# Six of nine tap products computed as even and odd halves with pairwise-summed weights

## The chip, the core and the metric

The kernel runs on one core of one Trainium2 chip. A core has a matrix engine (TensorE, PE in the profile, with its weight loads as PEld), two elementwise engines (VectorE, DVE; ScalarE, ACT), GpSimd (POOL), SyncE (SP), which here only issues DMAs, and 16 DMA engines that move data between the main memory and SBUF. PE writes its sums to PSUM, which has 8 banks of 128 x 512 float32; DVE and ACT read them from there. The metric is the device time of one execution in microseconds (us), lower is better.

## The reference

A causal dilated convolution over time with 15 taps and dilation 2, a gate, and a projection:

```python
B, T, D, K = (2, 4000, 512, 15)      # x: (B, T, D), w: (K, D, 2*D), w_o: (D, D), all bf16
pad = (K - 1) * 2
xp = jnp.pad(x, ((0, 0), (pad, 0), (0, 0)))
h = sum(einsum('btc,cd->btd', xp[:, pad - 2*i : pad - 2*i + T, :], w[i]) for i in range(K))
z = tanh(h[..., :D]) * sigmoid(h[..., D:])
out = z @ w_o
```

So each output row is a sum of 15 matrix products of 512 x 1024, then an elementwise gate, then one product of 512 x 512.

## The kernel before

**Streams.** Time is cut by its remainder modulo 8 into rows of 500 (NK): row r holds the times 8k + r. Because the dilation is 2, the even remainders (p = 0) and the odd ones (p = 1) never mix. A *supertile* is one batch entry and one p; there are 4. Inside it lie four streams U0 to U3, and the 15 taps fall into four phases of at most 4 taps (l = 0 to 3; tap 4l + e belongs to phase e, and tap 15 does not exist).

**Nine products.** A 4 x 4 polyphase filter would take 16 sub-filters. The kernel takes nine, by summing streams and weights first: a, b, c work on U0, U2, U02 = U0 + U2; d, e, f on U1, U3, U13; g, hh, ii on U01, U23, U0123. The weights for c, f, g, hh and ii are sums of taps, called slabs. The function `product` forms one of them in one PSUM bank: for each tap l and each 128-channel block cc one weight load and one matmul of 128 x 501 (500 columns and one more on the left), 16 in all; product e has three taps, 12. DVE combines the nine with additions and subtractions (p1, q1, A1, p2, q2, B1, s, s3, C0, qg, C1 and the four sums H0 to H3); ACT copies the products a, d, g from PSUM to SBUF first and later applies tanh (`th`) or sigmoid (`sg`).

**Loops.** The 512 channels of f and of g are done in four passes (dc) of 128 each, since the summed weights of more would not fit. In each pass the four supertiles follow each other, and each is done twice: hf = 0 gives the tanh half, hf = 1 the sigmoid half and z. One such piece is called a *unit* here: 4 passes x 4 supertiles x 2 halves = 32 units of 8 x 16 + 12 = 140 matmuls. In pass 0 the streams are made: by transposes on PE for the first supertile, by DMA transposes for the others, with four-row remainders by PE (`pt`); the five sums are made by DVE (line 219). They are written to main memory (`xsp`) and read back in passes 1 to 3. z is written to `zsp`; in the last pass `make_outproj_steps` reads it back and multiplies by w_o (`po`, line 353, 256 matmuls), ACT casts, SP stores.

**Weights.** `make_weight_steps` loads 15 taps per pass in two halves of 128 columns (128 KB each) and forms 18 summed slabs per half (line 151). For pass 0 POOL issues the loads and DVE adds; for passes 1 to 3 SP issues and POOL adds, all of it during the last unit of the pass before.

**What sets the order.** The code lists work per product and attaches the loads, sums and spills of the next supertile or pass as *hooks* behind a given product. When the program is built, a scheduler with its own costs orders the instructions of each engine; on the chip each engine then runs its own list strictly in that order and waits on semaphores. Tiles come from pools with a fixed number of buffers: a new tile waits until an old one has been read for the last time. What the change touches sits at `product` (line 258), the copies at lines 289, 300 and 321, `act_out` (lines 273 to 282), `produce_sum` (219), `reload` (223), the spill (240) and the hooks at the end.

Of the kernel before, what the change touches and what calls it, by code (L numbers as in the profile page):

```python
# [12 lines left out]
def kernel(  # L13
# [21 lines left out]
    assert K <= 16 and T % 8 == 0  # L35
# [8 lines left out]
    NREM = NK - NT16  # L44

# [34 lines left out]
    XORDER = [XNAME[pn] for pn in PRODS]  # L80

# [5 lines left out]
    wsl_pool = ctx.enter_context(tc.tile_pool(name="wsl", bufs=33 + 3))  # L87
    xin_pool = ctx.enter_context(tc.tile_pool(name="xin", bufs=9 + 2))
    pcopy_pool = ctx.enter_context(tc.tile_pool(name="pcopy", bufs=3))
    ctmp_pool = ctx.enter_context(tc.tile_pool(name="ctmp", bufs=3))  # L90
    keep_pool = ctx.enter_context(tc.tile_pool(name="keep", bufs=7))
    hpre_pool = ctx.enter_context(tc.tile_pool(name="hpre", bufs=3))
    th_pool = ctx.enter_context(tc.tile_pool(name="th", bufs=5))
    sg_pool = ctx.enter_context(tc.tile_pool(name="sg", bufs=2))
    z_pool = ctx.enter_context(tc.tile_pool(name="z", bufs=8))
# [3 lines left out]
    for (b, p) in supertiles:  # L99
        for n in XORDER:  # L100
            xsp[(b, p, n)] = dram.tile([P, CC, XU], bf16, name=f"xsp_{b}_{p}_{n}", tag=f"xsp_{b}_{p}_{n}")
# [23 lines left out]
    def make_weight_steps(dc, sum_eng, dma_eng):  # L125
        wo = {}
        slabs = {pn: [None] * NL for pn in PRODS}
        sums = {}
# [14 lines left out]
        def slab_add(pn, l, A, Bm, h):  # L143
            if A is None or Bm is None:
                slabs[pn][l] = A if Bm is None else Bm
                return
            if h == 0:
                t = wsl_pool.tile([P, CC, 2 * P], bf16, name=f"w{pn}{l}_p{dc}", tag="wsl")
                slabs[pn][l] = t
            t = slabs[pn][l]  # L150
            sum_eng.tensor_tensor(t[:, :, halfs(h)], A[:, :, halfs(h)], Bm[:, :, halfs(h)], ALU.add)  # L151

        def step_orig(pn, e):
            def fn(h):
                for l in range(NL):
                    load_orig(4 * l + e, h)
                    slabs[pn][l] = get_orig(4 * l + e)
            return fn

        def step_sum(pn, e0, e1):  # L160
            def fn(h):
                for l in range(NL):
                    slab_add(pn, l, get_orig(4 * l + e0), get_orig(4 * l + e1), h)
            return fn

        def step_ii(h):
            for l in range(NL):
                slab_add("ii", l, slabs["g"][l], slabs["hh"][l], h)
# [7 lines left out]
        return slabs, steps  # L176

    def make_x_steps(dc, b, p, sum_eng, use_dmat=False):
# [7 lines left out]
        def pe_rows(t, rows, k0, ksz, pt, slot, copy_eng):  # L186
            xn = xnat_pool.tile([P, D], bf16, name="xn", tag="xn")
            nc.sync.dma_start(xn[:ksz, :], rows[k0:k0 + ksz, :])  # L188
            for cc in range(CC):
# [6 lines left out]

        def produce_base(q):
# [279 lines left out]
```

## Time and profile before

| what | value |
|---|---|
| median of 4 runs | 1029.59 us (1028.81 to 1030.4) |
| the profiled execution's own time | 1029.43 us |
| its span (first to last instruction) | 1027.6 us |
| granted TensorE clock, mean | 0.999 |
| PE busy | 1016.1 us (99%), 4848 matmuls |
| DVE busy | 407.5 us (40%) |
| ACT busy | 177.0 us (17%) |
| POOL busy | 161.4 us (16%) |
| moved by DMA | 121.81 MB, 119 GB/s on the mean |

The span is the part that the trace shows; 1.83 us of the execution's time lie around it. In a row of the timeline the first number is the start in us from the span's start, the second how long the merged group lasted, then engine, line, operation, tiles and shape, and at the end the count. In a group's row the numbers behind the bar are the busy time of all in us, the mean of one in ns, and the idle time before them with what ended it. The duration of a matmul in the trace is a modelled one, from its start to when its result stands; matmuls overlap, so the pace of a stream is the difference of starts, not that duration.

### The profile page before, as it was taken

To read this page: it belongs to the slowest core of one execution; us is meant where nothing else is said; L and a number is where in the kernel's file an instruction comes from. 1 tells how busy PE (TensorE), PEld (TensorE's weight loads), DVE (VectorE), ACT (ScalarE), POOL (GpSimd) and SP (SyncE) were. 2 spreads that over 40 slices of the span, in tenths; PEclk is the share of its full clock that TensorE was granted. 3 is DMA by queue.
4 is the path that set the end of the run, shared out by engine and by line. 5 is a ranking of instruction groups with operands and counts; after the bars stand their busy time and mean duration, and the time that the engine had idled before them with its cause. 6 is when DMAs were issued, how large, how long until landed. Compare 5 with 4: busy or idle time off the path is not lost.

```text
span 1027.6 us, 12121 instructions
## 1 busy us (share of the span) xinstructions
PE 1016.1 (99%) x4848; PEld 472.2 (46%) x4848; DVE 407.5 (40%) x620; ACT 177.0 (17%) x298; POOL 161.4 (16%) x160
## 2 busy tenths in 40 slices
PE   6999999999999999999999999999999999999998
PEld 3444444444444444444444444444444544544444
DVE  3854443635533242433434343342544133223132
ACT  2111011111111111111011111111112312312214
POOL 8100000007900000004920000003850000000000
PEclk9999999999999999999999999999999999999999
DMA  9996672917543250608625060425615425323303
GB/s 241 233 227 97 152 134 62 230 26 175 159 123 88 62 144 21 164 22 185 175 81 161 23 182 2 134 73 138 191 42 148 137 62 156 108 84 104 98 1 95
DMA packets 174868, 121.81 MB, mean 119 GB/s; under 512 B 77276, under 2 KB 173852, under 8 KB 174812
## 3 DMA queue, kind: packets, MB, share of 16 engines
q1 hardware_dynamic: 173372, 117.11, 45.6%
q0 software_dynamic: 1440, 3.93, 1.5%
q8 instruction: 38, 0.62, 0.3%
q14 instruction: 18, 0.15, 0.0%
HBM read 81.56 MB, written 33.36 MB: 112 GB/s over the span
## 4 chain that ended last, share of the span: by engine, by line
PE 99%; DMA 1%; SPq 0%; ACT 0%; issue 0%
PE ps_a L258 11%; PE ps_c L258 11%; PE ps_b L258 11%; PE ps_f L258 11%; PE ps_d L258 11%; PE ps_hh L258 11%; PE ps_ii L258 11%; PE ps_g L258 11%; PE ps_e L258 8%; PE po L353 5%; PE pt L190 1%; DMA xn<-in_x_dram 1%; SPq L188 0%; ACT o_sb L360 0%
## 5 line engine op out<-in xcount | busy, mean ns | idle before, releaser
L258 PEld LDWEIGHTS <-wo_p 128*128 128x128 bf16 x2176 | 210.5, 97 | 248.9 <-issue 0.5
L258 PE MATMUL ps_a<-xU,wo_p 128*128 128x501 bf16 x512 | 114.3, 376 | 0.0
L258 PE MATMUL ps_c<-xU,wc_p 128*128 128x501 bf16 x512 | 114.2, 375 | 0.0
L258 PE MATMUL ps_d<-xU,wo_p 128*128 128x501 bf16 x512 | 114.2, 374 | 0.0
L258 PE MATMUL ps_b<-xU,wo_p 128*128 128x501 bf16 x512 | 113.9, 375 | 0.0
L258 PE MATMUL ps_ii<-xU,wii_p 128*128 128x501 bf16 x512 | 113.8, 374 | 0.0
L258 PE MATMUL ps_g<-xU,wg_p 128*128 128x501 bf16 x512 | 113.8, 374 | 0.0
L151 POOL TENSOR_TENSOR wc_p<-wo_p,wo_p 128x512 bf16<-128x512 bf16 x24 | 26.9, 1152 | 427.3 <-PE ps_b L258 426.4
L303 DVE TENSOR_TENSOR p<-d_sb,ps_e 128x500 f32<-128x500 f32 x32 | 21.7, 677 | 177.7 <-PE ps_e L258 177.7
L258 PE MATMUL ps_f<-xU,wf_p 128*128 128x501 bf16 x384 | 86.8, 375 | 0.0
L258 PE MATMUL ps_e<-xU,wo_p 128*128 128x501 bf16 x384 | 86.8, 375 | 0.0
L258 PE MATMUL ps_hh<-xU,whh_p 128*128 128x501 bf16 x384 | 86.8, 375 | 0.0
L292 DVE TENSOR_TENSOR p<-a_sb,ps_b 128x500 f32<-128x500 f32 x32 | 21.7, 677 | 148.9 <-PE ps_b L258 148.9
L273 ACT ACTIVATE th<-H 128x500 f32<-128x500 f32 x64 | 39.3, 620 | 224.9 <-DVE H L312 110.9
L277 ACT ACTIVATE sg<-H 128x500 f32<-128x500 f32 x64 | 39.3, 621 | 224.4 <-DVE H L312 117.4
L258 PEld LDWEIGHTS <-wg_p 128*128 128x128 bf16 x512 | 49.6, 97 | 59.0
L258 PEld LDWEIGHTS <-wii_p 128*128 128x128 bf16 x512 | 49.6, 97 | 59.0
L258 PEld LDWEIGHTS <-wc_p 128*128 128x128 bf16 x512 | 49.3, 97 | 57.8
L300 ACT COPY d_sb<-ps_d 128x501 f32<-128x501 f32 x32 | 18.5, 577 | 280.0 <-PE ps_d L258 280.0
L324 DVE TENSOR_TENSOR C<-g_sb,ps_hh 128x500 f32<-128x500 f32 x32 | 21.7, 677 | 92.2 <-PE ps_hh L258 92.1
L279 DVE TENSOR_TENSOR zt<-th,sg 128x500 bf16<-128x500 f32 x64 | 48.5, 777 | 24.1 <-ACT sg L277 23.4
L258 PEld LDWEIGHTS <-whh_p 128*128 128x128 bf16 x384 | 37.2, 97 | 44.3
(48 smaller groups left out, 763.0 us busy)
## 6 DMA issues: line engine op xcount, KB each, us to landing
xU<-xsp_U SPq DMA_DIRECT2D x108, 516.0 KB
xsp_U<-xU SPq DMA_DIRECT2D x36, 516.0 KB
wo_p<-in_w_dram SPq DMA_DIRECT2D x90, 128.0 KB
zsp<-zt SPq DMA_DIRECT2D x48, 125.0 KB
zl<-zsp SPq DMA_DIRECT2D x48, 125.0 KB
out_dram<-o_sb SPq DMA_DIRECT2D x32, 126.0 KB
wo_p<-in_w_dram POOLq DMA_DIRECT2D x30, 128.0 KB, 7.3
out_dram<-o_sb SPq DMA_DIRECT2D x16, 128.0 KB
```

The source lines that it names most:

```text
L151: sum_eng.tensor_tensor(t[:, :, halfs(h)], A[:, :, halfs(h)], Bm[:, :, halfs(h)], ALU.add)
L190: nc.tensor.transpose(pt[:, slot, cc, 0:ksz], xn[:ksz, cc * P:(cc + 1) * P], ident[:ksz, :ksz])
L258: nc.tensor.matmul(ps[:, :], lhsT=slabs[pn][l][:, cc, hf * P:(hf + 1) * P], rhs=xtile[:, cc, st:st + NP1], start=(idx == 0), stop=(idx == ...
L273: nc.scalar.activation(th[:], H[:, K1], AF.Tanh)
L277: nc.scalar.activation(sg[:], H[:, K1], AF.Sigmoid)
L279: V.tensor_tensor(zt[:], state["th"][q][:], sg[:], ALU.mult)
L292: V.tensor_tensor(r["p1"][:, K1], r["a_sb"][:, K1], ps[:, KSH], ALU.add)
L300: nc.scalar.copy(r["d_sb"][:, ALLC], ps[:, ALLC])
L303: V.tensor_tensor(r["p2"][:, K1], r["d_sb"][:, K1], ps[:, KSH], ALU.add)
L324: V.tensor_tensor(r["C0"][:, K1], r["g_sb"][:, K1], ps[:, KSH], ALU.add)
L353: nc.tensor.matmul(po[:ksz, :], lhsT=zs[dcp][:, k0:k0 + ksz], rhs=wo_sb[:, dcp, :], start=(dcp == 0), stop=(dcp == HC - 1),)
```

## The change

Six of the nine products (a, c, d, f, g, ii) are no longer 16 matmuls of 501 columns. Each stream they use is split again, by the parity of k, into three half-length pieces kept in one tile of the pool `xh`: `o` (the odd-indexed columns), `m` (even minus the odd one after) and `n` (even minus the odd one before). Their taps are grouped in pairs, and the sums of two neighbouring taps are new slabs (`slabs2`, tiles with `_2` in the name). A split product is then three pieces of 2 taps x 4 blocks = 8 matmuls of 251 columns:

1. the pair sums times `o`, into bank ps_o; ACT copies it to SBUF (`u_h`);
2. taps 0 and 2 times `n`, into bank ps_e; DVE adds `u_h` and writes every other column of the result;
3. taps 1 and 3 times `m`, added onto ps_o where it stands (so the first matmul of this piece must wait until ACT has read ps_o); ACT copies the sum to the other columns.

The products b, e and hh stay as they were, and so do all nine in the very first unit. With the split go these edits: for c, f and ii the combining operations now read SBUF instead of PSUM; `th` and `sg` are bf16; s and s3 are written in place; s is formed later. The halves are made in pass 0 (two copies by ACT and two subtractions by DVE for each of six streams), are what is spilled and reloaded (756 KB instead of 516 KB for those six), and have one buffer per stream. The summed slabs of passes 1 to 3 are added by DVE and no longer by POOL, and the second halves of loads and sums move from the last unit of a pass to the first unit of the next one. Spills of pass 0 move to hf = 0. Pools shrink (xin 11 to 7, keep 7 to 4, z 8 to 6, zld 9 to 6, and the output tile is one of 5 small ones instead of one of 4 with four parts) and the weight pool grows (36 to 47).

```diff
+    NKH = NK // 2
+    NH1 = NKH + 1
+    HALO2 = 2
+    XH = HALO2 + NKH
+    SPLIT = ("a", "c", "d", "f", "g", "ii")
...
-    wsl_pool = ctx.enter_context(tc.tile_pool(name="wsl", bufs=33 + 3))
-    xin_pool = ctx.enter_context(tc.tile_pool(name="xin", bufs=9 + 2))
+    wsl_pool = ctx.enter_context(tc.tile_pool(name="wsl", bufs=33 + 2 * NSPL + 2))
+    xin_pool = ctx.enter_context(tc.tile_pool(name="xin", bufs=(9 - NSPL) + 4))
+    xh_pool = ctx.enter_context(tc.tile_pool(name="xh", bufs=NSPL + XH_SPARE)) if NSPL else None
...
+        def pair_sums(pn, h):
+            if pn not in SPLIT:
+                return
...
+            for hh_ in hs:
+                for lam in range(NL // 2):
+                    slab_add(slabs2, pn, lam, slabs[pn][2 * lam], slabs[pn][2 * lam + 1], hh_)
...
+        def produce_halves(n):
+            nat = xt[n]
+            base = HALO - 2 * HALO2
+            new_halves(n)
+            to, tm, tn = xt[n + "o"], xt[n + "m"], xt[n + "n"]
+            nc.scalar.copy(to, nat[:, :, base + 1:base + 2 * XH:2])
+            nc.scalar.copy(tm, nat[:, :, base:base + 2 * XH - 1:2])
+            nc.gpsimd.memset(tn[:, :, 0:1], 0.0)
+            sum_eng.tensor_tensor(tn[:, :, 1:XH], tm[:, :, 1:XH], to[:, :, 0:XH - 1], ALU.subtract)
+            sum_eng.tensor_tensor(tm, tm, to, ALU.subtract)
...
+        def half_mms(ps, taps, xtile, first):
+            mm = [(lam, cc) for lam in range(len(taps)) if taps[lam] is not None for cc in range(CC)]
+            for idx, (lam, cc) in enumerate(mm):
+                st = HALO2 - 1 - lam
+                nc.tensor.matmul(
+                    ps[:, :],
+                    lhsT=taps[lam][:, cc, hcols],
+                    rhs=xtile[:, cc, st:st + NH1],
+                    start=(first and idx == 0),
+                    stop=(idx == len(mm) - 1),
+                    skip_group_check=(not first),
+                )
+
+        def split_product(pn, dst):
+            n = XNAME[pn]
+            sl = slabs[pn]
+            ps_o = ps_pool.tile([P, NH1], f32, name=f"ps_{pn}_o", tag="bank")
+            half_mms(ps_o, slabs2[pn], xt[n + "o"], True)
+            u_h = hsb_pool.tile([P, NH1], f32, name="u_h", tag="hsb")
+            nc.scalar.copy(u_h[:, :], ps_o[:, :])
+            ps_e = ps_pool.tile([P, NH1], f32, name=f"ps_{pn}_e", tag="bank")
+            half_mms(ps_e, [sl[0], sl[2]], xt[n + "n"], True)
+            V.tensor_tensor(dst[:, 1:NP1:2], ps_e[:, 1:NH1], u_h[:, 0:NKH], ALU.add)
+            half_mms(ps_o, [sl[1], sl[3]], xt[n + "m"], False)
+            nc.scalar.copy(dst[:, 0:NP1:2], ps_o[:, :])
...
-                th = th_pool.tile([P, NK], f32, name="th", tag="th")
+                th = th_pool.tile([P, NK], bf16, name="th", tag="th")
...
-                sg = sg_pool.tile([P, NK], f32, name="sg", tag="sg")
+                sg = sg_pool.tile([P, NK], bf16, name="sg", tag="sg")
...
-                        nxt_slabs, nwsteps = make_weight_steps(dc + 1, nc.gpsimd, nc.sync)
+                        nxt_wts, nwsteps = make_weight_steps(dc + 1, nc.vector, nc.sync)
...
-                            add_hook(pi, nwsteps[1][pi])
+                        deferred_g = nwsteps[1]
...
+                if hf == 0 and si == 0 and dc > 0 and deferred_g is not None:
+                    for pi in range(NPR):
+                        add_hook(pi, deferred_g[pi])
...
-                emit_unit(dc, b, p, hf, slabs, xt, state, hooks)
+                emit_unit(dc, b, p, hf, wts, xt, state, hooks, use_split=not first_unit)
```

Two places show how the lists of the engines move. The first is ACT in pass 1, first supertile, second half, from product d or f to the product a of the next unit. Before:

```order
L300 COPY d_sb<-ps_d 128x501
L277 ACTIVATE sg<-H_2647 128x500
L277 ACTIVATE sg<-H_2654 128x500
L321 COPY g_sb<-ps_g 128x501
L277 ACTIVATE sg<-H_2707 128x500
L277 ACTIVATE sg<-H_2735 128x500
L289 COPY a_sb<-ps_a 128x501
```

and with the change:

```order
L369 COPY u_h<-ps_f_o 128x251
L374 COPY f_sb<-ps_f_o 128x251
L369 COPY u_h<-ps_g_o 128x251
L386 ACTIVATE sg<-H_3525 128x500
L386 ACTIVATE sg<-H_3532 128x500
L374 COPY g_sb<-ps_g_o 128x251
L369 COPY u_h<-ps_ii_o 128x251
L386 ACTIVATE sg<-H_3597 128x500
L374 COPY ii_sb<-ps_ii_o 128x251
L369 COPY u_h<-ps_a_o 128x251
L386 ACTIVATE sg<-H_3639 128x500
L374 COPY a_sb<-ps_a_o 128x251
```

The copy `u_h` of g stands ahead of the two sigmoids that wait for DVE's H0 and H2, and the copy `u_h` of the next a ahead of the last sigmoid. The second place is DVE late in the very first unit, before the operation C (line 324, later 449) that reads product hh. Before (`wii`, `wf`, `wg`, `whh` are slabs of pass 0):

```order
L151 TENSOR_TENSOR wii_p_567<-wg_p_499,wo_p_282 128x4x128
L151 TENSOR_TENSOR wf_p_452<-wo_p_396,wo_p_425 128x4x128
L151 TENSOR_TENSOR wf_p_454<-wo_p_398,wo_p_427 128x4x128
L151 TENSOR_TENSOR wf_p_456<-wo_p_400,wo_p_429 128x4x128
L151 TENSOR_TENSOR wg_p_493<-wo_p_247,wo_p_396 128x4x128
L151 TENSOR_TENSOR wg_p_495<-wo_p_249,wo_p_398 128x4x128
L151 TENSOR_TENSOR wg_p_497<-wo_p_251,wo_p_400 128x4x128
L151 TENSOR_TENSOR wg_p_499<-wo_p_253,wo_p_402 128x4x128
L151 TENSOR_TENSOR whh_p_526<-wo_p_276,wo_p_425 128x4x128
L324 TENSOR_TENSOR C_553<-g_sb,ps_hh 128x500
```

and with the change (two more rows of `wc_2` follow before C):

```order
L269 TENSOR_TENSOR xU_0_0_0_565<-xU_0_0_0_478,xU_0_0_0_531 128x4x516
L164 TENSOR_TENSOR whh_4_p_573<-wo_p_294,wo_p_455 128x4x128
L164 TENSOR_TENSOR whh_4_p_575<-wo_p_296,wo_p_457 128x4x128
L164 TENSOR_TENSOR whh_4_p_577<-wo_p_298,wo_p_459 128x4x128
L164 TENSOR_TENSOR wc_4_p_361<-wo_p_259,wo_p_294 128x4x128
L164 TENSOR_TENSOR wc_4_p_363<-wo_p_261,wo_p_296 128x4x128
L164 TENSOR_TENSOR wc_4_p_365<-wo_p_263,wo_p_298 128x4x128
L164 TENSOR_TENSOR wc_4_p_367<-wo_p_265,wo_p_300 128x4x128
L164 TENSOR_TENSOR wc_2_p_583<-wc_4_p_361,wc_4_p_363 128x4x128
L279 TENSOR_TENSOR xU0123h_0_0_567<-xU0123h_0_0_567 128x4x251
L164 TENSOR_TENSOR wc_2_p_585<-wc_4_p_365,wc_4_p_367 128x4x128
L280 TENSOR_TENSOR xU0123h_0_0_567<-xU0123h_0_0_567 128x1008
```

Before, all five slab sums of the first half, `wii` included, stand ahead of C, so that product ii has its weights early; with the change pair sums (`wc_2`) and the subtractions that make the halves (L279, L280) have moved in, and `wii` stands behind C.

More of the change, by code (lines that the diff above doesn't have):

```diff
@@ L235, in step, with halves, fn @@
             return fn
+        def halves(n):
+            def fn():
+                if dc == 0 and n in XSPLIT:
+                    produce_halves(n)
+            return fn
+        def step(n):
+            def fn():
+                main(n)()
+                halves(n)()
+            return fn
         def spill(n):
@@ L295, in emit_unit @@
             elif pn == "c":
+                if "c" in SPLIT and use_split:
+                    ps = to_sbuf("c", "c_sb")
+                else:
+                    ps = product(pn)
                 r["A1"] = ftile(keep_pool, "A1")
@@ L330, in emit_unit @@
             elif pn == "ii":
+                if "ii" in SPLIT and use_split:
+                    ps = to_sbuf("ii", "ii_sb")
+                else:
+                    ps = product(pn)
                 r["C1"] = ftile(ctmp_pool, "C1")
```

201 lines of the change are left out of this document (141 added, 60 removed).

## The prediction

> **What bounds the kernel now.** I read the page first: busy shares, the clock, and the chain of waits by engine.
>
> ```profile
> PE 1016.1 (99%) x4848; PEld 472.2 (46%) x4848; DVE 407.5 (40%) x620; ACT 177.0 (17%) x298; POOL 161.4 (16%) x160
> PEclk9999999999999999999999999999999999999999
> PE 99%; DMA 1%; SPq 0%; ACT 0%; issue 0%
> ```
>
> PE is the bound from end to end, at full clock, and nothing but the first load is ahead of it. So the change pays by what it takes from PE's stream, as long as no other engine becomes late. The second view is the timeline of PE and of its weight loads in the first unit:
>
> ```profile
> 18.63 0.64 PEld L190 LDWEIGHTS <-xn 128*128 128x128 bf16 x8
> 18.84 0.61 PE L190 MATMUL pt<-ident,xn 128*128 128x128 bf16 x8
> 19.28 0.59 PE L258 MATMUL ps_c<-xU,wc_p 128*128 128x501 bf16 x2
> ...
> 33.79 3.56 PE L258 MATMUL ps_g<-xU,wg_p 128*128 128x501 bf16 x16
> 37.19 2.71 PE L258 MATMUL ps_hh<-xU,whh_p 128*128 128x501 bf16 x12
> ```
>
> Product g starts at 33.79 and hh at 37.19: 16 pairs of weight load and matmul in 3.40 us, 212.5 ns each. Eight transposes, also one weight load each but only 128 columns, take 19.28 - 18.84 = 0.44 us, 55 ns each. So the pace follows the columns, and almost no fixed part is left.
>
> **The matmuls: -155 us.** The line through (128, 55) and (501, 212.5) has 0.422 ns per column and gives 251 columns 55 + 123 x 0.422 = 107 ns. Bounds: half of 212.5 (no fixed part) is 106, and 212.5 if the time did not fall at all. I take 107, since both rows lie on the line. A split product then takes 24 x 0.107 = 2.57 us instead of 3.40, 0.83 less; 6 products x 31 units = 186 of them, 186 x 0.83 = 154.8 us. A unit is 6 x 2.57 + 2 x 3.40 + 2.55 (e, 12 matmuls) = 24.8 us instead of 29.75.
>
> The weights must keep up: 24 loads instead of 16, one every 107 ns. The eight loads above, 128 columns each, took 0.64 us in all; less than 0.64 / 8 = 80 ns apart, so a load can come faster than it is needed.
>
> [...]
>
> **The new wait: nothing by itself.** The third piece may only start when ACT has copied the first one out of the same bank. The rows:
>
> ```profile
> 11.59 4.01 PE L258 MATMUL ps_a<-xU,wo_p 128*128 128x501 bf16 x16
> 15.64 0.58 ACT L289 COPY a_sb<-ps_a 128x501 f32<-128x501 f32 x1 [4.87 <-PE ps_a L258]
> 19.26 1.07 ACT L193 COPY xU<-pt 128x512 bf16<-128x512 bf16 x2 [3.04 <-PE pt L190]
> L190 PE MATMUL pt<-ident,xn 4*128 4x4 bf16 x48 | 3.0, 163 | 0.0
> L289 ACT COPY a_sb<-ps_a 128x501 f32<-128x501 f32 x32 | 18.4, 576 | 41.2 <-PE ps_a L258 41.2
> L258 PE MATMUL ps_a<-xU,wo_p 128*128 128x501 bf16 x512 | 114.3, 376 | 0.0
> ```
>
> ACT starts 0.04 us after the modelled end of the last matmul (11.59 + 4.01 = 15.60). A matmul of 4 columns is modelled at 163 ns and one of 501 at 376, so 251 columns are about 270 ns. The first piece ends at 7 x 0.107 + 0.27 = 1.02 us. The copy of 501 elements takes 0.576; two of 512 follow each other within 1.07 - 0.585 = 0.485, so an element costs at most 0.95 ns. For 251 the ends are 0.29 (half) and 0.576 (no gain); 250 elements at nearly that rate are some 0.21 to 0.24 less than 0.576, I take 0.36. Then ACT is done at 1.02 + 0.04 + 0.36 = 1.42, and the third piece is due at 16 x 0.107 = 1.71 us: 0.29 to spare, 0.07 at the upper end. The cover is the second piece. If ACT is late, each 0.1 us beyond the spare costs 186 x 0.1 = 19 us. What could be ahead of it on ACT, in order, are the activations, each of which waits for DVE. The rows of ACT in the changed program put `u_h` of g ahead of the two activations of H0 and H2; behind it only the copies of g and the `u_h` of ii wait, and that one is due after all of hh (3.40 us) as well. So DVE may be some 3 us late before PE feels it.
>
> **DVE in an ordinary unit** has room:
>
> ```profile
> 101.42 0.68 DVE L324 TENSOR_TENSOR C<-g_sb,ps_hh 128x500 f32<-128x500 f32 x1 [4.29 <-PE ps_hh L258]
> 102.01 0.67 DVE L326 TENSOR_TENSOR qg<-g_sb,ps_hh 128x500 f32<-128x500 f32 x1
> 26.02 3.51 DVE L219 TENSOR_TENSOR xU<-xU,xU 128x2064 bf16<-128x2064 bf16 x3
> 40.06 1.44 DVE L151 TENSOR_TENSOR wg_p<-wo_p,wo_p 128x512 bf16<-128x512 bf16 x4
> 25.00:47.00 22.00, 22.00 (x108) 10.13 (x107) 21.73 (x46) 3.17 (x6) 3.31 (x7) 1.00 0.98 226
> ```
>
> A 500-element float32 operation occupies 0.59 us (102.01 - 101.42), a slab sum (1.44 - 0.43) / 3 = 0.335, a 2064-element bf16 sum (3.51 - 1.23) / 2 = 1.14. The combining of `ps_e` has 250 elements: between 0.30 (half) and 0.59, I take 0.33. A unit has 15 x 0.59 + 6 x 0.33 = 10.8 us; z in bf16 adds 4 x 0.33 to 0.59 in a second half, 12.2. Against 24.8 of PE this hides wholly.
>
> **The start: +12 us.** The last row, the window from 25 to 47 us (columns: PE, PEld, DVE, ACT, POOL, clock, DMA share, GB/s), shows DVE busy 21.73 of 22 us: in the first unit it is as tight as PE. There the change adds 12 pair sums per half, 24 x 0.335 = 8.0 us, and 12 subtractions of some 1000 elements, each 0.6 at the rate of line 219 (2064 in 1.14) or 1.1 at the rate of the float32 operations (500 in 0.59). I take 1.1 for `n` and 0.6 for `m`: 10.2 us. The order of DVE shows where it hurts: the slabs of ii now stand behind C, which needs hh. Going down that list, g waits some 4.5 us for its slabs and ii some 4 more, and the second unit then starts 8 to 9 us late; a few us more follow since DVE ends the pair sums at about 62 us, where the bank of the second unit's first `ps_e` comes free. I take 12; the bounds are 0 (all 18 us find the gaps that DVE has before 25 us) and 18.
>
> [...]
>
> **The rest of pass 0: +4 us.** In three more second halves DVE has 12.2 + 5 sums x 1.14 + 10.2 = 28.1 us for 24.8 of PE, 3.3 over in each; ACT has 12 more copies of 1008. The bank of a product is reused about 8 allocations later, half a unit, so most is absorbed and repaid in the next first half (10.8 us). I take 4 for all; bounds 0 and 10.
>
> **Changes of pass: +4 us.** The 18 slab sums and 12 pair sums per half, now on DVE, are 30 x 0.335 = 10.1 us; 12.2 + 10.1 = 22.3, still under 24.8. But DVE, in order, also waits there for loads, which SP issues one by one:
>
> ```profile
> 47.78 6.58 SPq L138 DMA_DIRECT2D wo_p<-in_w_dram  x6
> 820.00:850.00 30.00, 30.00 (x143) 13.71 (x142) 9.55 (x15) 4.18 (x7) 0.00 (x0) 1.00 0.25 69
> ```
>
> 1.1 us each, 30 x 1.1 = 33 us of SP over two units of together 50, with reloads between; the sums for c come just as c's operations are due. I take 1.3 us each for three changes; bounds 0 and 4 each. The second row is an ordinary unit of the last pass: DMA share 0.25, DVE 9.55 of 30, so nothing else is near its limit there, and 50% more bytes for six reloads fit.
>
> **Last pass: +3 us.** The 256 `po` matmuls stay. ACT casts them in between; a `u_h` due behind a cast (0.585) may be 0.3 to 0.5 late, about twice in each of three units. Bounds 0 and 8.
>
> **Sum** against the profiled execution: span 1027.6 - 154.8 + 12 + 4 + 4 + 3 = 895.8, with 1.8 around it 897.6; the median before lies 0.16 over that execution. I predict 898 us.
>
> **Rivals.**
>
> *The pace does not follow the columns (slower).* If a weight load could not hide behind 107 ns of matmul, 24 loads are worse than 16. For it: 97 ns per load (the mean in the group below) is nearly all of 107. Against it: the eight transposes at 55 ns. It decides from a pace of 3.40 / 24 = 142 ns, with the 23 us of stalls from 137. If load and matmul followed each other, 204 ns, 24 x 0.204 = 4.90, +1.50 each, 186 x 1.50 = +279: 1331 us. Chance 3%.
>
> ```profile
> L258 PEld LDWEIGHTS <-wg_p 128*128 128x128 bf16 x512 | 49.6, 97 | 59.0
> ```
>
> *The third piece waits every time.* If the copy takes 0.576 and the release some 0.1 to 0.2 more than I count, 0.1 to 0.4 us are lost on each split product; at 0.25, 186 x 0.25 = 46: 944 us. For it: the spare is only 0.29. Against it: ACT is 17% busy and starts 0.04 after its input. Chance 15%.
>
> *DVE is the bound wherever weights and streams are made.* If strided writes and reads cost double and its waits for loads hold up ACT's activations, the start is 20, the three units of pass 0 are 5 each, the changes of pass 5 each: 20 + 15 + 15 + 3 = 53, 30 more than the sum: 928 us. Chance 17%.
>
> *All of it hides.* Only some 5 us at the start remain: 898 - 18 = 880 us. Chance 15%.
>
> **How the numbers follow.** My forecast, 888 to 912, has 50%; the rivals 3, 15, 17 and 15%. The range leaves out half of the last (below 878) and the upper part of the wait and the slower case (above 945): 878 to 945. A change of 0.2% is about what can be told from none here. Faster 0.96, same 0.01, slower 0.03.
>
> **What would show it.** Right: starts of 251-column matmuls 107 ns apart, a unit of the middle passes in 24.8 us, no idle time of PE put down to `u_h`, and PE idle for some 12 us before 75 us, released by DVE (slabs or `ps_e`). Wrong: pieces spaced wider than 115 ns; a gap ahead of each third piece; idle PE around the changes of pass, released by DVE's line 164 or by DMA; DVE busy over 90% of units outside the first two.

## The result: 1029.9 us before, 897.3 us after

| | before | after |
|---|---|---|
| median of runs | 1029.91 us (12 runs, 1028.81 to 1030.76) | 897.31 us (8 runs, 895.61 to 898.58) |
| ratio after / before | | 0.871, 95% interval 0.8705 to 0.8722 |
| span of the profiled execution | 1027.6 us | 895.1 us |
| length of an undisturbed unit | 29.71 us | 24.99 us |

The kernel became 13% faster; 898 us was forecast. The terms of that sum did not all hold, as the traces show below. The page of the kernel after (busy shares, the chain of waits by engine):

```profile
PE 873.7 (98%) x6336; PEld 617.9 (69%) x6336; DVE 529.9 (59%) x1058; ACT 303.3 (34%) x625; POOL 27.5 (3%) x76
PE 89%; DVE 7%; issue 1%; ACT 1%; DMA 1%; SPq 0%; DVEq 0%; ACTq 0%
```

PE is still the bound, but DVE has entered the chain with 7%. Three quarters of that lie in the first 100 us, as will be seen. First a split product in a middle pass, on PE and on ACT (line 354 is `half_mms`, 341 `product`, 369 the copy `u_h`):

```profile
507.64 1.03 PE L354 MATMUL ps_ii_o<-xU0123h,wii_p 128*128 128x251 bf16 x8
508.51 1.03 PE L354 MATMUL ps_ii_e<-xU0123h,wii_p 128*128 128x251 bf16 x8
509.38 1.03 PE L354 MATMUL ps_ii_o<-xU0123h,wii_p 128*128 128x251 bf16 x8
```
```profile
508.77 0.37 ACT L369 COPY u_h<-ps_ii_o 128x251 f32<-128x251 f32 x1 [3.59 <-PE ps_ii_o L354]
```

Three pieces start 0.87 us apart, eight matmuls in each: 108.7 ns per matmul of 251 columns. `u_h` runs from 508.77 to 509.14, the third piece starts at 509.38, so 0.24 us were to spare and PE has no gap (0.30 us in d, f and g, where ACT starts 0.04 us after the modelled end of the piece and not 0.10). A unit of 16 + 16 + 12 undivided matmuls and six such products takes 24.99 us. Two windows of the length of a unit in the second pass (columns: PE, PEld, DVE, ACT, POOL, clock, DMA share, GB/s) show how much room DVE has. The first is the pass's first unit, in which the slabs of the second half are made and DVE has no room at all; the other is an ordinary one:

```profile
232.69:257.67 24.98, 24.98 (x191) 18.24 (x189) 24.98 (x64) 6.71 (x16) 0.00 (x0) 1.00 0.74 202
275.00:300.00 25.00, 25.00 (x191) 18.27 (x189) 13.33 (x25) 6.87 (x16) 0.00 (x0) 1.00 0.52 153
```

Now the places where PE does wait. In the first two units, on PE:

```profile
34.80 1.02 PE L341 MATMUL ps_g<-xU,wg_p 128*128 128x501 bf16 x4 [0.69 <-DVE wg_p L164]
36.32 1.02 PE L341 MATMUL ps_g<-xU,wg_p 128*128 128x501 bf16 x4 [0.49 <-DVE wg_p L164]
39.01 1.87 PE L341 MATMUL ps_g<-xU,wg_p 128*128 128x501 bf16 x8 [1.67 <-DVE wg_p L164]
...
47.47 5.25 PE L341 MATMUL ps_ii<-xU,wii_p 128*128 128x501 bf16 x16 [3.07 <-DVE wii_p L164]
...
80.58 1.03 PE L354 MATMUL ps_ii_o<-xU0123h,wii_p 128*128 128x251 bf16 x8 [1.77 <-ACT u_h L369]
```

The weights of g are 2.85 us late in all, those of ii 3.07. And ii then takes over 5 us where an undivided product takes 3.40: the clock was lowered after the idle time. The windows around it have 1.00 for the clock, then 0.65:

```profile
44.00:47.00 3.00, 0.40 (x2) 0.00 (x0) 3.00 (x8) 0.00 (x0) 0.00 (x0) 1.00 0.88 332
47.00:50.00 3.00, 2.53 (x7) 0.97 (x8) 3.00 (x11) 0.62 (x1) 0.00 (x0) 0.65 1.12 228
```

On DVE in that moment, the sums of ii stand behind a combination that needed all of hh:

```profile
46.38 0.70 DVE L453 TENSOR_TENSOR H<-C,p 128x500 f32<-128x500 f32 x1
46.97 1.11 DVE L164 TENSOR_TENSOR wii_p<-wg_p,whh_p 128x512 bf16<-128x512 bf16 x3
```

The 1.77 us at 80 us have a cause that the prediction did not have. On ACT the two copies that make halves for the next supertile stand ahead of `u_h`, and the first of them waited 3.14 us for a sum of DVE:

```profile
78.28 1.04 ACT L276 COPY xU01h<-xU 128x1008 bf16<-128x1008 bf16 x1 [3.14 <-DVE xU L269]
79.22 1.03 ACT L277 COPY xU01h<-xU 128x1008 bf16<-128x1008 bf16 x1
80.16 0.36 ACT L369 COPY u_h<-ps_ii_o 128x251 f32<-128x251 f32 x1
```

At the changes of pass little is lost; on PE these are all gaps over 0.15 us there:

```profile
260.24 1.03 PE L354 MATMUL ps_a_o<-xU0h,wo_p 128*128 128x251 bf16 x8 [0.67 <-ACT u_h L369]
441.75 1.03 PE L354 MATMUL ps_c_o<-xU02h,wc_p 128*128 128x251 bf16 x8 [0.45 <-ACT u_h L369]
462.01 1.03 PE L354 MATMUL ps_a_o<-xU0h,wo_p 128*128 128x251 bf16 x8 [1.12 <-ACT u_h L369]
662.45 1.03 PE L354 MATMUL ps_a_o<-xU0h,wo_p 128*128 128x251 bf16 x8 [0.38 <-ACT u_h L369]
```

What makes `u_h` late there is on DVE and on ACT:

```profile
255.11 1.12 DVE L164 TENSOR_TENSOR wii_p<-wg_p,whh_p 128x512 bf16<-128x512 bf16 x3
...
258.29 0.71 DVE L453 TENSOR_TENSOR H<-C,p 128x500 f32<-128x500 f32 x1
```
```profile
259.03 0.62 ACT L382 ACTIVATE th<-H 128x500 bf16<-128x500 f32 x1 [2.49 <-DVE H L453]
...
259.81 0.37 ACT L369 COPY u_h<-ps_a_o 128x251 f32<-128x251 f32 x1
```

DVE is busy without a break in the first unit of the pass, its slab sums stand ahead of H, the activation waits for H, and `u_h` of the next product stands behind the activation. The other three gaps have the same order on the two engines, and the first units of the passes 2 and 3 keep DVE as full (25.00 us busy in the 25 from 434.5 and in the 25 from 635).

### The profile page after: what moved, and what is told of

Read it like the earlier page. It is cut to its first block, busy times and chain, and to the rows that moved or that the text cites. A ratio compares the mean times of both kernels' runs of the same rounds, so it can differ in the third digit from the quotient of the medians.

```text
span 895.1 us, 16197 instructions
## 1 busy us (share of the span) xinstructions
PE 873.7 (98%) x6336; PEld 617.9 (69%) x6336; DVE 529.9 (59%) x1058; ACT 303.3 (34%) x625; POOL 27.5 (3%) x76
## 4 chain that ended last, share of the span: by engine, by line
PE 89%; DVE 7%; issue 1%; ACT 1%; DMA 1%; SPq 0%; DVEq 0%; ACTq 0%
PE ps_b L341 11%; PE ps_hh L341 11%; PE ps_e L341 8%; PE po L481 6%; PE ps_c_o L354 6%; PE ps_d_o L354 6%; PE ps_ii_o L354 6%; PE ps_f_o L354 6%; PE ps_a_o L354 6%; PE ps_g_o L354 5%; PE ps_d_e L354 3%; PE ps_f_e L354 3%; PE ps_c_e L354 3%; PE ps_ii_e L354 3%; PE ps_g_e L354 3%; PE ps_a_e L354 3%
## 5 line engine op out<-in xcount | busy, mean ns | idle before, releaser
L354 PEld LDWEIGHTS <-wii_p 128*128 128x128 bf16 x744 | 72.3, 97 | 16.8 <-issue 1.9
L354 PEld LDWEIGHTS <-wc_p 128*128 128x128 bf16 x744 | 72.1, 97 | 16.0 <-issue 1.0
L354 PEld LDWEIGHTS <-wf_p 128*128 128x128 bf16 x620 | 60.3, 97 | 13.5
L354 PE MATMUL ps_ii_o<-xU0123h,wii_p 128*128 128x251 bf16 x496 | 64.0, 271 | 1.8 <-ACT u_h L369 1.8
L354 PE MATMUL ps_c_o<-xU02h,wc_p 128*128 128x251 bf16 x496 | 64.0, 271 | 0.6 <-ACT u_h L369 0.6
L354 PE MATMUL ps_g_o<-xU01h,wg_p 128*128 128x251 bf16 x496 | 63.9, 271 | 0.0
L382 ACT ACTIVATE th<-H 128x500 bf16<-128x500 f32 x64 | 39.3, 620 | 50.6 <-DVE H L453 19.6
L386 ACT ACTIVATE sg<-H 128x500 bf16<-128x500 f32 x64 | 39.0, 620 | 38.8 <-DVE H L453 15.7
L481 PE MATMUL po<-wo_sb,zl 128*126 128x512 bf16 (+1 forms) x192 | 51.9, 379 | 0.0
L354 PE MATMUL ps_f_o<-xU13h,wf_p 128*128 128x251 bf16 x372 | 50.5, 271 | 0.0
L489 ACT CAST o_sb<-po 128x512 bf16<-128x512 f32 (+1 forms) x64 | 37.4, 586 | 32.6 <-PE po L481 29.3
```

What stands on the lines that cost most here:

```text
L354: nc.tensor.matmul(ps[:, :], lhsT=taps[lam][:, cc, hcols], rhs=xtile[:, cc, st:st + NH1], start=(first and idx == 0), stop=(idx == len(mm) ...
L382: nc.scalar.activation(th[:], H[:, K1], AF.Tanh)
L386: nc.scalar.activation(sg[:], H[:, K1], AF.Sigmoid)
L481: nc.tensor.matmul(po[:ksz, :], lhsT=zs[dcp][:, k0:k0 + ksz], rhs=wo_sb[:, dcp, :], start=(dcp == 0), stop=(dcp == HC - 1),)
L489: nc.scalar.copy(o_sb[:ksz, :], po[:ksz, :])
```

## Experiments

Diffs are against the kernel after the change. In each text "before" and "after" are the two kernels of this document. A unit's length is read from PE's timeline, from the first matmul of a to the next.

**e1: half of the cover.** What hides `u_h`?

```diff
             nc.scalar.copy(u_h[:, :], ps_o[:, :])
+            half_mms(ps_o, [sl[1], sl[3]], xt[n + "m"], False)
+            nc.scalar.copy(dst[:, 0:NP1:2], ps_o[:, :])
             ps_e = ...; half_mms(ps_e, ...); V.tensor_tensor(dst[:, 1:NP1:2], ...)
-            half_mms(ps_o, [sl[1], sl[3]], xt[n + "m"], False)
-            nc.scalar.copy(dst[:, 0:NP1:2], ps_o[:, :])
```

> Everything as in the change, but the third piece of each split product is written ahead of the second; in the order of TensorE only four matmuls of the second piece are left between the first and the third. Theory (the copy u_h is hidden only by the second piece): after the change the third piece starts 16 x 0.1085 = 1.736 us into a product and u_h is ready 0.24 us earlier, at 1.50; with four matmuls as cover it is due at 12 x 0.1085 = 1.30, so 0.20 us are lost in each of 186 products: +37 us, about 934 us, with idle time of TensorE put down to u_h ahead of nearly every third piece. Rival (the bank comes free when the first piece is done, the copy is not on the path): 897 us and no such idle time.

Measured: 929.8 us (ratio to before 0.903, 0.901 to 0.905). A steady unit takes 26.24 us, 1.25 more, 0.21 per split product. PE and ACT in product g:

```profile
518.85 1.03 PE L354 MATMUL ps_g_o<-xU01h,wg_p 128*128 128x251 bf16 x8
519.72 0.60 PE L354 MATMUL ps_g_e<-xU01h,wg_p 128*128 128x251 bf16 x4
520.34 1.03 PE L354 MATMUL ps_g_o<-xU01h,wg_p 128*128 128x251 bf16 x8
```
```profile
519.92 0.37 ACT L369 COPY u_h<-ps_g_o 128x251 f32<-128x251 f32 x1 [0.92 <-PE ps_g_o L354]
```

The third piece starts 1.49 us into the product, 0.05 after `u_h` ends at 520.29; 1.50 was expected. So the copy is on the path, and only the second piece hides it. The idle time is in the spacing of starts; since ends of matmuls are modelled, the profile attaches no wait to it. The whole is 32.5 us instead of 37, because places that already waited do not pay twice: the second and the third unit lose 0.3 us each.

**e2: three products.**

```diff
-    SPLIT = ("a", "c", "d", "f", "g", "ii")
+    SPLIT = ("c", "f", "ii")
```

> Only c, f and ii are split; a, d and g are computed as before the change. Theory (each split product takes 24 x 0.1085 = 2.604 us where the undivided one takes 3.40, all else is small): 3 x 0.796 x 31 = 74 us come back; of the stall in the first two units, which is pair sums and subtractions for six, up to half (5 us) goes: 966 to 971 us, a steady unit of 24.99 + 2.39 = 27.38 us. Rival (the gain per unit is not made by the pace alone, for instance the unit was also held up by VectorE before): a steady unit that is not 27.38 us.

Measured: 955.4 us (0.928, 0.926 to 0.930). The steady unit is 27.35 us, as the pace says. But the whole is 11 us better than expected: the first four units lose little. Without any stall they would take 32.39 (the first unit before the change) + 3 x 27.35 + 1.2 for the small transposes in two of them (0.58 each), 115.6; they took 117.5. With six products the same count is 108.5, and they took 120.8. So the loss at the start is not shared evenly among the products. In the first two units DVE is busy for 55.5 us here, where PE alone would need 60.3, and for 59.6 with six products, where PE would need 58.0. That fits a loss that begins when DVE is full, without proving it.

**e3: twice as many matmuls, half as wide.** How far does the pace follow the columns?

```diff
-            for idx, (lam, cc) in enumerate(mm):
-                nc.tensor.matmul(ps[:, :], ..., rhs=xtile[:, cc, st:st + NH1], ...)
+            for c0, c1 in ((0, 126), (126, NH1)):
+                for idx, (lam, cc) in enumerate(mm):
+                    nc.tensor.matmul(ps[:, c0:c1], ..., rhs=xtile[:, cc, st + c0:st + c1], ...)
```

> Each matmul of 251 columns in a split product is made as two of 126 and 125 columns, each with its own weight load; same sums. Theory (the time of a matmul goes by its columns, as on the line through 128 columns at 55 ns, 251 at 108.5 and 501 at 212.5): two of them take 54 + 54 = 108 ns, the time stays at 897 us. Rival (a weight load of 128 columns takes at least 80 ns, the spacing that eight loads in a row were counted at, and this is hidden behind 108 ns but not behind 54): 160 instead of 108.5 ns, 24 x 0.0515 x 186 = +230 us, about 1127 us.

Measured: 905.2 us (0.879, 0.878 to 0.881), 8 more than expected; a steady unit takes 25.31 us, 0.32 more. This kernel, with two column ranges in one bank, does not compute the reference's sums (relative error 0.48; why is not shown); number and kind of its instructions are as described. On PE:

```profile
520.56 1.05 PE L355 MATMUL ps_c_o<-xU02h,wc_p 128*128 128x126 bf16 x16
521.45 1.05 PE L355 MATMUL ps_c_e<-xU02h,wc_p 128*128 128x126 bf16 x16
```

16 in 0.89 us, 56 ns each with a weight load of its own, where 54 were expected. The load is hidden even there (from 520 to 545 us PE is busy for all of the 25.00, with 331 loads), and the rival falls: the 80 ns that the prediction read off eight loads are no lower bound, only the most that those eight were apart.

**e4: the size of the spare.** One more copy of the first piece ahead of `u_h`.

```diff
+            nc.scalar.copy(dst[:, 0:NP1:2], ps_o[:, :])
             nc.scalar.copy(u_h[:, :], ps_o[:, :])
```

> One more copy of the first piece on ScalarE ahead of u_h (into the even columns of the result, which the later copy overwrites), so that u_h is ready 0.28 to 0.38 us later. Theory (0.24 us is spare): the third piece starts 0.04 to 0.14 us late in each of 186 products, +7 to +26 us, 905 to 923 us. Rival (the spare read off the trace is not real, since ends of matmuls are modelled): no change at 897 us if the spare is over 0.4 us, and +52 to +71 us (950 to 968) if there is none.

Measured: 901.6 us (0.876, 0.875 to 0.878), a little under the 905 to 923 expected: +0.02 us per split product (a unit of 25.13). ACT, where line 369 is now the extra copy and 370 `u_h`, and PE's third piece:

```profile
520.68 0.39 ACT L369 COPY d_sb<-ps_d_o 128x251 f32<-128x251 f32 x1 [0.43 <-PE ps_d_o L354]
520.96 0.36 ACT L370 COPY u_h<-ps_d_o 128x251 f32<-128x251 f32 x1
```
```profile
521.38 0.81 PE L354 MATMUL ps_d_o<-xU1h,wo_p 128*128 128x251 bf16 x6
```

`u_h` of d is 0.28 us later and the price is 0.02, so some 0.25 us could be used up. The trace has 0.30 for d, less the 0.05 by which a waiting piece starts behind the copy (e1): 0.25. On the mean over the six products the trace gives 0.22 in this way; e1, four matmuls of cover (0.43) for 0.21 lost, gives the same. The spare read off the trace is real.

**e5: the second half's weights later.** Is the loss at the start one of order?

```diff
-                    GLAG = 4
+                    GLAG = 7
```

> In the first unit the weights of the second half (their loads, slab sums and pair sums) are emitted seven products behind those of the first half instead of four; the same work, in another order on VectorE: the sums for a and c of the second half no longer stand ahead of the slabs of g and ii. Theory (the stall of the first unit is one of order: ii waits 3.07 us, then runs 1.7 us slower on a lowered clock, because its sums stand behind the combinations that wait for hh; g waits 2.85 us, of which 1.34 are the pair sums of a): -3.07 - 1.7 - 1.3 = about -6 us, 891 us, the first unit about 36 us, and no loss in the second unit, since its banks run out only 13.8 us after its start. Rival (VectorE is simply full, the amount of work counts and not its order): the second unit loses what the first gains, 896 to 899 us.

Measured: 897.7 us (0.872, 0.870 to 0.873): no change, the rival was right. The first unit fell from 41.86 to 36.74 us, the second rose from 24.99 to 32.42. What the theory had missed is on PE at 61 us:

```profile
61.53 1.84 PE L354 MATMUL ps_d_e<-xU1h,wo_p 128*128 128x251 bf16 x8 [2.71 <-DVE a_sb L372]
```

DVE does all sums of the second half ahead of the combination `a_sb`. In the kernel after it reaches `a_sb` at 60.97 us, here at 61.07: the same work ends at the same time, whatever its order.

**e6: twelve pair sums out of the first unit.** In addition to e5, the pair sums of the first half (first read in the third unit) are made at the end of the second unit and in the third.

```diff
-            if defer_pairs:
-                if h == 0: return
-                hs = (0, 1)
+            if pn not in SPLIT or (defer_pairs and h == 0 and not late): return
...
+                if dc == 0 and si == 0 and hf == 1:
+                    for pj in range(4): add_hook(8, wsteps[2][pj])
+                if dc == 0 and si == 1 and hf == 0:
+                    for pj in range(4, NPR): add_hook(pj - 4, wsteps[2][pj])
```

> As the run with later second halves, and the twelve pair sums of the first half, which are first read in the third unit, leave the first unit: those of a, b-free c and d are made at the end of the second unit, the others inside the third. Theory of order: most of the stall is gone already by the order, and this brings 0 to 2 us more: 889 to 891 us. Rival (amount of VectorE's work in the first two units): 12 x 0.335 = 4 us less than the run with later second halves.

Measured: 893.7 us (0.868, 0.867 to 0.870), 4.0 less than e5, which is the rival's number. But it does not wholly hold: the third unit now waits 2.47 us for the pair sums of a.

**e7: seven products.** b is split too. Not shown are the halves of U2, which are made with the others, and one or two buffers less in four pools (streams, input rows, reloads of z, output tiles).

```diff
-    SPLIT = ("a", "c", "d", "f", "g", "ii")
+    SPLIT = ("a", "b", "c", "d", "f", "g", "ii")
```

> Product b is split too (seven of nine); to make room, the slabs have 47 buffers for 14 pair sums instead of 47 for 12, natural streams 6 instead of 7, and the input rows, z reloads and output tiles one or two less. Theory (each split product is worth 3.40 - 2.605 = 0.795 us wherever VectorE has room): 31 x 0.795 = -24.6 us, with +2 to +6 for one more pair of subtractions and four more sums in the crowded first two units: 875 to 879 us, a steady unit of 24.20 us. Rival (VectorE or ScalarE becomes the bound, as b is followed at once by c and d, all split, with p1, q1 and A1 waiting on them; or the missing buffers make reloads late): a steady unit over 24.6 us, 885 us or more.

Measured: 883.4 us (0.858, 0.857 to 0.859), 14 us better than after, 10.7 short of the 24.6; the rival's 885 or more did not come either. Steady units are 24.20 as expected. The second to the eighth unit take 180.2 us together, against 180.1 after the change: no gain at all there, which is 5.6 of the 10.7. In pass 0 PE now waits in each second half, for `u_h` of g and of ii, and ACT's list shows why:

```profile
128.58 1.03 PE L354 MATMUL ps_g_o<-xU01h,wg_p 128*128 128x251 bf16 x8 [0.24 <-ACT u_h L369]
132.06 1.03 PE L354 MATMUL ps_ii_o<-xU0123h,wii_p 128*128 128x251 bf16 x8 [0.38 <-ACT u_h L369]
```
```profile
127.24 1.02 ACT L277 COPY xU1h<-xU 128x1008 bf16<-128x1008 bf16 x1
128.17 0.36 ACT L369 COPY u_h<-ps_g_o 128x251 f32<-128x251 f32 x1
```

`u_h` follows at once on a copy of halves: there ACT's queue is what is late. DVE is busy for 39.5 of the 50.7 us of these two units. About 3 us more are lost at the changes of pass, where PE waits 0.91 to 1.41 us for `u_h` of c, and about 2 in the last pass, where its longest waits, 0.34 and 1.25 us, are for reloads of z: the missing buffers may have a part in that.

**e8: weight sums of passes 1 to 3 back on POOL.**

```diff
-                        nxt_wts, nwsteps = make_weight_steps(dc + 1, nc.vector, nc.sync)
+                        nxt_wts, nwsteps = make_weight_steps(dc + 1, nc.gpsimd, nc.sync)
```

> The slab sums and pair sums of passes 1 to 3 go back to GpSimd, where the slab sums were before the change; all else as in the change. Theory (these had to be moved: 60 sums at a change of pass at the 1.27 us that one took on GpSimd before are 76 us, from about 18 us ahead of the pass, so they end about 58 us into it, while the sums of ii for the second half are due 47 us into it): 5 to 12 us lost at each of three changes, 912 to 933 us, TensorE waiting for GpSimd's line 164. Rival (the move hides nothing, the sums are early enough on either engine): 897 us, or 2 to 3 us less since VectorE's queue is free of them at the changes of pass.

Measured: 926.9 us (0.900, 0.898 to 0.902), 30 us lost. PE waits for POOL, in the second unit of a pass:

```profile
278.50 0.61 PE L354 MATMUL ps_f_o<-xU13h,wf_p 128*128 128x251 bf16 x4 [3.30 <-POOL wf_p L164]
```

So moving these sums to DVE was a necessary part of the change. The first three units of the second pass take 26.99, 32.45 and 26.39 us where they took 24.99, 25.82 and 24.99. That the place is f and not ii differs from what was expected.

**e9 and e10: POOL takes work from DVE in pass 0.** With e5's order, the pair sums of the first half and most of the subtractions of lines 279 and 280 run on POOL; e9 with six split products, e10 with seven.

```diff
-            sum_eng.tensor_tensor(tn[:, :, 1:XH], ...)
-            sum_eng.tensor_tensor(tm, tm, to, ALU.subtract)
+            e_n = nc.gpsimd if (not first or n in ("U01", "U0123")) else sum_eng
+            e_n.tensor_tensor(tn[:, :, 1:XH], ...)
+            e_n.tensor_tensor(tm, tm, to, ALU.subtract)
```

> Six products split as in the change. In pass 0 VectorE is relieved: the pair sums of the first half are made on GpSimd during the second unit, both subtractions of U01h and U0123h of the first stream set and of every product of the other sets go to GpSimd, and the weights of the second half are emitted seven products behind those of the first half. Theory (the loss of 13 us in the first four units is VectorE's amount of work: 4 us of it taken out of the first unit brought 3.6): 4.0 us of pair sums and 4 x 0.6 of subtractions less before the third unit bring about 6, the 0.8 us in each of the fourth, sixth units go too: 888 to 891 us. Rival (subtractions of 1004 elements take over 2.5 us on GpSimd and are late for the next unit, or slow VectorE down): 894 us or more, TensorE waiting for GpSimd.

> The run with seven split products and the relief of VectorE in pass 0 together. Theory (of the 24.5 us that the seventh split is worth, 11 were lost because pass 0 is full on VectorE: units of 26.2 instead of 24.2 us; with the relief these are back): 888 to 891 less 24.5, and up to 3 for the changes of pass: 864 to 870 us. Rival (what was lost was in ScalarE's queue, u_h behind the copies of halves, and in the missing buffers): little more than the relief alone brings with six, 876 to 880 us.

Measured: 942.7 us (0.915, 0.914 to 0.917) and 955.8 us (0.928, 0.926 to 0.929). Both lose some 45 and 72 us against the kernels they were built from (897.7 and 883.4). The theory's side was wrong, and the reason is on DVE and POOL at the same time:

```profile
87.22 0.41 DVE L369 TENSOR_TENSOR g_sb<-ps_g_e,u_h 128x250 f32<-128x250 f32 x1
87.55 2.23 DVE L432 TENSOR_TENSOR H<-p,B 128x500 f32<-128x500 f32 x1
89.70 2.55 DVE L435 TENSOR_TENSOR H<-A,p 128x500 f32<-128x500 f32 x1
92.18 2.57 DVE L437 TENSOR_TENSOR p<-p,p 128x500 f32<-128x500 f32 x1
```
```profile
89.25 2.47 POOL L276 TENSOR_TENSOR xU13h<-xU13h 128x1004 bf16<-128x1004 bf16 x1
...
91.80 2.41 POOL L277 TENSOR_TENSOR xU13h<-xU13h 128x1008 bf16<-128x1008 bf16 x1
```

DVE's operations with both inputs in SBUF take 2.23 to 2.57 us instead of 0.67, and step in time with POOL's (two of them start at 89.70 and 92.18, 0.45 and 0.38 behind POOL's two); the one that reads one input from PSUM (`g_sb`) takes its usual 0.41. It was to be seen in the trace of before too, where POOL made the sums at the changes of pass:

```profile
277.33 1.62 DVE L315 TENSOR_TENSOR H<-A,p 128x500 f32<-128x500 f32 x1
```

In that whole trace the 27 operations of this shape that had a sum of POOL beside them took 1.26 us on the mean, the 165 others 0.68, and with an input from PSUM it was 0.67 to 0.68 in both cases. There it lay in DVE's spare time and cost nothing. In e9 it reaches PE by way of ACT, whose sigmoids wait for the slow H, with a copy of halves and `u_h` behind them:

```profile
89.82 0.62 ACT L383 ACTIVATE sg<-H 128x500 bf16<-128x500 f32 x1 [4.18 <-DVE H L432]
...
93.74 0.36 ACT L366 COPY u_h<-ps_ii_o 128x251 f32<-128x251 f32 x1
```
```profile
94.16 1.86 PE L351 MATMUL ps_ii_o<-xU0123h,wii_p 128*128 128x251 bf16 x8 [6.18 <-ACT u_h L366]
```

The granted clock is lower too, 0.978 and 0.968 on the mean (0.994 and 0.999 in e5 and e7), which is a part of the loss: behind the idle 6.18 us the next pieces in e9 start 1.65 and 1.68 us apart instead of 0.87. So GpSimd is no relief for DVE here.

**e11 and e12: halves made where they are read.** As e6, and the halves of U01 and U0123 are made in the unit that reads them first; e11 with six split products, e12 with seven.

```diff
+    LATE_HALVES = ("U01", "U0123")
...
+                if dc == 0 and hf == (1 if si == 0 else 0):
+                    add_hook(0, nxs["halves"]["U01"])
+                    add_hook(2, nxs["halves"]["U0123"])
```

> Six split products, no sums or subtractions on GpSimd. As the run with pair sums later, and the halves of U01 and U0123 (two ScalarE copies and two VectorE subtractions each) are made in the unit that reads them first, instead of in the one before, which is the fuller one. Theory (pass 0 loses by VectorE's amount of work in the second half of each set, 3 us over what a unit holds): 4 x 0.6 = 2.4 us of VectorE leave the first unit and each of the three other crowded ones: 2 us from the first units and about 1 from the later ones, 889 to 892 us against 893.7. Rival (the loss there is one of ScalarE's queue, u_h behind the copies of halves that wait for VectorE): the copies now stand in the unit in which u_h is due, 894 us or more.

> Seven split products with the same two changes of order. Theory (as above): 883.4 for seven in the old order, less 3.6 for the pair sums and 3 to 7 for the late halves (units of pass 0 at 24.2 to 25 us instead of 26.2): 873 to 877 us. Rival (what the seventh split lost in pass 0 has another cause, ScalarE's queue or missing buffers): 879 to 881 us.

Measured: 896.2 us (0.870, 0.868 to 0.871) and 879.7 us (0.854, 0.853 to 0.855). The rivals' numbers came out in both, in e11 for another reason than the rival's. There the first unit is down to 33.96 us, but the third starts late, on PE and on DVE:

```profile
78.70 1.95 PE L351 MATMUL ps_a_o<-xU0h,wa_p 128*128 128x251 bf16 x8 [6.49 <-DVE wa_p L165]
```
```profile
77.90 0.41 DVE L369 TENSOR_TENSOR ii_sb<-ps_ii_e,u_h 128x250 f32<-128x250 f32 x1
78.23 0.42 DVE L165 TENSOR_TENSOR wa_p<-wo_p,wo_p 128x512 bf16<-128x512 bf16 x1
```

A sum of 0.42 us, free of any wait on PE, stands behind the combination of ii at the end of DVE's list for that unit: my placing of the pair sums of a. The later units of pass 0 (25.8 to 26.1 and 25.2 us in turn) did not change. Of the 1.0 us by which a pair of them exceeds 2 x 24.99 in the kernel after, 0.57 are the small transposes of the stream remainders (before the change, in four groups and not one, 1.14); the rest are three short waits of third pieces, too short for the profile to name: the pieces ahead of them, in d, g and a, last 1.01, 0.96 and 1.07 us instead of 0.87. In e12 the units of pass 0 are as in e7 (24.5 and 26.1), with the same two waits of PE (0.24 and 0.38 us). The copies that stand ahead of `u_h` there are those of U1 and U13, which this edit does not move, so e12 neither relieves ACT's queue at that place nor tests it. About half of e12's 3.7 us gain over e7 lies in the first three units, 93.8 instead of 95.6 us. e12 is the fastest version, 2% below the kernel after.

## Why the prediction was right, and where it was not

The number came out within 1 us, and that is luck: the gain of the matmuls was put 8.5 us too high and the four losses together 9 us too high, and the two cancelled. In spans: 1027.6 - 895.1 = 132.5.

| term | predicted | measured |
|---|---|---|
| matmuls | -154.8 | 31 x (24.99 - 29.71) = -146.3 |
| the wait for `u_h` in ordinary units | 0 | 0, with 0.25 to 0.30 us to spare (0.29 predicted) |
| start (the first three units) | +12 | +10.6 |
| rest of pass 0 | +4 | about 0 |
| changes of pass | +4 | +3.3 |
| last pass | +3 | +0.3, all at its end |

**The matmuls.** Right in mechanism: the pace follows the columns, now also shown at 126 (56 ns) and 251 (108.7). Mis-sized: 107 ns was taken; 1.7 ns more on 24 x 186 matmuls are 7.6 us, and most of the rest is the undivided product, which took 3.394 and not 3.40. The rival on pace fell with it: even at 56 ns per pair the weight loads stay hidden.

**The new wait.** Right in an ordinary unit, and the best supported step: the trace, e1 and e4 agree within some 0.03 us on what could be used up. `u_h` took 0.37 (0.36 taken), ACT started 0.04 to 0.10 after the modelled end (0.04 taken). The prediction named what could be ahead of it on ACT, "in order, are the activations, each of which waits for DVE", and so left out the copies of halves, which stand in the same list and wait for DVE. They made the 1.77 us at 80 us, and they stand ahead of the waits in pass 0 with seven products (e7, e12). The prediction also looked at `u_h` of g and of ii only; that of the next a stands behind one more activation, and there PE waited at each of the three changes of pass. So its sign "no idle time of PE put down to `u_h`" held in the ordinary units and not at these places.

**The start.** Right in place and nearly in size, less so in its parts. g waited 2.85 (4.5 predicted), ii 3.07 (4), and a lowered clock added 1.7 that was not foreseen; the second unit's first product started at 52.56 instead of 43.98, 8.6 us late (8 to 9 predicted). The 2.0 us that followed in the next two units came mostly from ACT's copies, not from the bank of the first `ps_e`. The subtractions of `n`, which write from the second bf16 element on, were put at 1.1 us, the rate of the float32 operations (500 elements in 0.59); this was an estimate, and no run shows 1.1 for them. They took what those of `m` take, on DVE:

```profile
70.04 0.68 DVE L279 TENSOR_TENSOR xU1h<-xU1h 128x1004 bf16<-128x1004 bf16 x1
...
71.23 0.68 DVE L280 TENSOR_TENSOR xU02h<-xU02h 128x1008 bf16<-128x1008 bf16 x1
```

All 24 of `n` and all 24 of `m` took 0.67 to 0.70 us. So an output that starts 2 bytes off did not cost anything here, and 3 of the 18 us of added DVE work fall away. As to the cause: e2 shows that three products lose 1.9 us where six lose 12, e5 that another order alone gains nothing, e6 that 4 us of DVE's work moved out of the first unit, half of it behind the second, gain 4.0. e11 contradicts a plain count of work, since 2.4 us less in the first unit only let the stall grow at the third. What is shown is that the loss moves with where DVE's work stands in the first three units; which order loses least is open.

**Rest of pass 0, last pass.** Both were costed from the busy shares of DVE and ACT (28.1 of 24.8 us of DVE in three units). Neither loss came in that size with six products. DVE's work is spread over two units, busy for 21.1 of 25.8 us and for 16.8 of 25.2, and PE waits 0.45 us in such a pair:

```profile
105.67:131.48 25.81, 25.81 (x207) 18.64 (x205) 21.12 (x38) 15.51 (x26) 0.58 (x5) 1.00 0.50 163
131.48:156.67 25.19, 25.15 (x191) 18.26 (x189) 16.75 (x31) 8.99 (x19) 0.63 (x5) 1.00 0.68 184
```

That the table has about 0 is because the transposes, now in one group, save 0.57 us in each pair. With seven products PE waits 1.8 us in a pair.

**Changes of pass.** Nearly right in size, only in part in mechanism. DVE was put at 22.3 of 24.8 us, with its loss coming from waits for loads. It was busy for all of the 25.0 us, which is one of the signs of being wrong that the prediction named (over 90% outside the first two units), and ahead of the gaps at 260, 462 and 662 us it had not waited for a load for over 25 us. What PE felt was the chain from slab sums by way of H and the activation to `u_h`. With seven products, in units 0.8 us shorter, the loss there doubled (e7). Ahead of the gap at 441.75 DVE did wait 1.18 us for a load, 9 us earlier; what part that has is open.

**Rivals.** "The third piece waits every time" would have been 944; e1 shows what it looks like, 929.8, once the cover is 0.4 us shorter. "DVE is the bound" would have been 928; in the trace DVE has 7% of the chain: it was the bound in the first units and, just, in the first unit of each later pass, and nowhere else. "All of it hides" would have been 880; the first three units alone lost 10.6.

## What to carry to other kernels

A matmul on half the columns with its own weight load cost about half here (212.2, 108.7 and 56 ns at 501, 251 and 126 columns), so the algebraic split paid (0.871 of the time before) where the additions found room; what decided was the elementwise engines' queues at the places where streams and weights are made. A wait that is hidden has a size: read it as the start of the waiting instruction less the end of what it waits for, and take the cover away once to see it. Before work goes from VectorE to GpSimd, look for VectorE operations with two SBUF inputs in the trace while GpSimd is at work: here they took 1.26 us beside it and 0.68 alone before the change, and in e9 the move relieved nothing and lost 45 us.

## What was not expected of the hardware

- VectorE's operations with two SBUF inputs took 2.23 to 2.57 us beside GpSimd's subtractions, 0.67 alone (500 float32 elements, e9); `g_sb`, with one input from PSUM, 0.41 in both cases.
- An idle time of 3.07 us on TensorE was followed by a lowered clock (0.65 in the window behind it) in the kernel after, but in e7, after the same 3.07 us, the clock stayed at 1.00 (47 to 53 us) and ii took 3.57 us instead of 5.25. What makes the two executions differ is not shown.
- A weight load with its matmul of 126 columns came every 56 ns (e3).
